# A planned packed attention and ELU feed-forward kernel: stores that count as due late, dearer accumulating stores and weight loads in the plan, a fourth weight buffer, and an order chosen anew

## The chip, the cores and the metric

The kernel runs on one core of one Trainium2 chip. The metric is the device time in microseconds (us) of one execution. A core has TensorE (PE; its weight loads are shown apart as PEld), VectorE (DVE), ScalarE (ACT), GpSimd (POOL) and SyncE (SP), each with a queue of instructions of its own that it works off in order, and sixteen DMA engines that move what the queues issue.

## The reference

There are 8 batches of 8 heads, 576 tokens, head size 64, 32 packed rows `p` a head; the feed-forward part has model size 512 and inner size 2048 over all 4608 tokens.

```python
def sm_attn(qq, kk, vv):
    s = scale * np.matmul(qq, kk.transpose(0, 1, 3, 2))
    s = s - np.max(s, axis=-1, keepdims=True)
    a = np.exp(s)
    a = a / (np.sum(a, axis=-1, keepdims=True) + 1e-09)
    return np.matmul(a, vv)
p_packed = sm_attn(p, k, v)
out = sm_attn(q, p_packed, p_packed)
...
x = out.transpose(0, 2, 1, 3).reshape(B * S, H * D)
h = x @ w_in
g = np.where(h > 0.0, h, alpha * (np.exp(np.minimum(h, 0.0)) - 1.0))
return (g @ w_out).astype(np.float32)
```

All values are float32. The kernel splits them into a high and a low part and multiplies high by high, high by low and low by high.

## The kernel before

**The work.** For each batch the kernel computes the scores of the packed rows against the keys (the "first scores"), their softmax, the product with the values (`psum<-kvq,tmp` on PE, L663), and the scores of the queries against the packed rows (L708, the "second scores"). Those are turned by DVE's 32x32 transposes (the fold, L716), go through the second softmax, and are turned back (the unfold, L758). Since the attention's output is a small matrix times the packed rows, the kernel multiplies the packed rows into `w_in` first (L809, giving `m_hi` and `m_lo`), and a token's `h` is the second softmax (`a_hi`, `a_lo`, or `q` where the unfold writes whole values) times `m`.

**The feed-forward part.** It goes over steps of a batch, a window of its tokens (256 or 320) and one of 16 blocks of 128 inner columns. A step has 12 matmuls or 6 for `h` (L1306, L1313), ELU on ACT and DVE (`e`, `g`; L1320 is its relu, L1326 its exp), and an "out group" of six matmuls with `w_out` (L1409 to L1412), whose operand has a high and a low part in `wo_a` (blocks 0 to 7) or `wo_b` (blocks 8 to 15). In batches 0 and 1 the windows are visited several times, four blocks at a time, before all weights are there. The first visit's sum is stored in `out` by SyncE; later ones are added to it by GpSimd's DMA (`accum_op`, L1455, the accumulating stores). From batch 2 on two blocks are worked off together by seven products instead of eight, which need sums of weights: these are made once (L932 to L970), stored in `sw_dram`, and loaded again for each pair (L1158), four loads of 256 KB a set. `S_PLAINS` lists the pairs that are worked off plainly, with no sums. The last 64 tokens of a batch are kept in `hb`, stored in `rest_dram` (L998) and worked off at the end.

**The weights.** A block of `w_in` or `w_out` comes as 64-bit floats, 512 KB, into a buffer of the ring `raw` (L347, SyncE). ACT lifts the uppermost bits of the low word (`up<-raw`, L342), copies them in place (`top<-up`, L320), and DVE puts the float32 word together ("whole", L367). For `w_out`, ACT then casts to the high part (`wo_a<-raw`, `wo_b<-raw`) and DVE subtracts for the low one (L381); this last one releases the buffer. There are three buffers, and L320 is the line of all casts and copies.

**What sets the order.** No order is written out. Each piece of work is an `op` with a due time (`prio`, in steps), what it costs on each engine that can do it, what it depends on, and the buffers that it takes. `schedule()` plays this forward in time: it takes the op with the earliest due time that is ready, whose buffers are free, and whose engine is idle, and writes it down. The sequence in which ops were taken is each engine's program. `"DMA"` stands for SyncE's queue and `"POOL"` for GpSimd's. The chip then goes through these programs, with semaphores where one waits for another. So a cost in the plan takes no time; it only moves instructions. The tables `T_...`, `LI`, `LO`, `LM`, `LOOK`, `TM` shift the due times of kinds of ops: `T_ATT...` those of the attention's parts, `T_SL` the loads of weight sums (due `i - T_SL` for the step `i` that uses them), `T_SE` the final sums and stores of `out`, `T_HS` the stores of `rest_dram`, `T_SW` the making of the sums.

K, v and q of batches 1 to 7 share one ring, `kvq`, of two buffers: k's two halves, then v's, then q's, each of which is loaded when the one two before it has been used.

Of the kernel before, what the change touches and what calls it, by code (L numbers as in the profile page):

```python
# [16 lines left out]
U8 = mybir.dt.uint8  # L17
# [6 lines left out]
def packed_attention_elu_ffn(  # L24
# [58 lines left out]
    ]  # L83
    T_ATT = [11.5, 5.0, 17.5, 8.0, 10.0, 14.0]
    T_ATT1 = [-17.0, -14.5, -14.0, -6.0, -18.5, -13.0]
    LI = 4.0
    LO = 2.0
    LM = 1.0
    LOOK = 4.25
    TM = [26.5, 32.5, 37.5, 36.5]  # L90
    FIRST = "q v i3 k i0 i1 i2 o2".split()
    COLD = 1.9
    T_S2 = -8.0
    STAY = 19
    SWITCH = 0.105
    F_PLAIN = 0
    H_PLAIN = [0, 1]
    T_WS = 11
    T_AS = 6
    S_PLAIN = []  # L100
    S_PLAINS = {
        (2, 0): [7], (2, 1): [0], (3, 0): [1], (3, 1): [0], (4, 0): [0, 4], (4, 1): [1],
        (5, 0): [0], (5, 1): [0], (6, 0): [4], (6, 1): [7],
    }
    T_SW7 = 36
    T_ATTS = {3: [-2.5, -1.5, -5.5, 8.5, 12.0, 21.0], 4: [-1.5, 7.5, 13.5, 3.5, 10.0, 23.0], 5: [-6.5, 4, -10.5, -3.5, 12.5, 28.0], 6: [5, 10, 14.0, 3.5, 11.5, 24.5], 7: [1.0, -10, -5, 3.5, 11.5, 23.0]}
    TMS = {3: [19, 30.0, 34.5, 30.0], 4: [22, 19.5, 26.0, 27.0], 5: [11.5, 28.5, 29.0, 29.0], 6: [23, 18.5, 28.0, 23.0], 7: [16.5, 35, 30.0, 31.5]}
    T_RL = 21.0
    T_RX = 2.0
    T_HS = 20.5  # L110
    S_FIRST = (2, 0)
    T_SW = 7.5
    T_SL = 6.5
    T_SE = 15.0
    LOOK_S = 5.5
# [54 lines left out]

    def op(prio, on, fn, deps=(), take=(), use=(), after=(), mode=None, lag=0):
        o = Op()
        o.lag = lag
        o.prio, o.on, o.fn, o.deps = prio, on, fn, [d for d in deps if d is not None]
        o.after = [d for d in after if d is not None]
        o.take, o.end, o.n, o.mode = list(take), None, len(ops), mode
        for b in list(take) + list(use):
            b.users.append(o)
        ops.append(o)
        return o  # L180

    def schedule():
# [25 lines left out]
        while todo:  # L208
            for n, o in enumerate(todo[:400]):
# [21 lines left out]
                for x, needs in o.next:  # L231
                    x.wait -= 1
                    if needs:
                        x.ready = max(x.ready, o.end)
                for r in {id(b.ring): b.ring for b in o.take}.values():
# [5 lines left out]
            else:  # L241
                ends = [o.end for o, _ in out[-400:] if o.end > now]
                ends += [t for t in idle_at.values() if t > now]
# [45 lines left out]
    for x in top_ts:  # L289
# [4 lines left out]
        kvq=2, m_hi=NFC, m_lo=NFC, a=2, tmp=3, g=3, e=2, h=2, sw=SW, w8=2, hb=HB,  # L294
        raw=3, up=2, top=TOP, p=2, ppT=2, pp=1, k0=1, q0=1,
    ).items()}
# [33 lines left out]
    def weights(f, first, prio):  # L330


        raw = ring_tile("raw", stg, [P, 8 * WC + 8], U8, "raw", bufs=3)
        up_b = ring_tile("up", stg, [P, WC], U16, "up")
# [51 lines left out]
        t = FIRST.index(name) - 60 if name in FIRST else prio - 8  # L386
        ld = op(t, {"DMA": 1.45}, load, take=[raw])
        x = op(prio, {"ACT": 0.63, "DVE": 0.42}, lift, [ld], take=[up_b], use=[raw])
# [28 lines left out]
    def attention(b, ts):  # L417
# [65 lines left out]
        def load_v(e, n):  # L483
            x = v_b[n].t
            nc.sync.dma_start(
                out=x[:, :2 * E].rearrange("p (c e) -> p c e", c=2),
                in_=v[b, 2 * n * P:2 * (n + 1) * P, :].rearrange("(c p) e -> p c e", p=P),
            )
            nc.sync.dma_start(
                out=x[:S - 4 * P, 2 * E:], in_=v[b, 4 * P:, n * E // 2:(n + 1) * E // 2]  # L490
            )

# [431 lines left out]
    def strassen_weights(u):  # L924
# [35 lines left out]
        for n, b in enumerate(sw):  # L960
            def high(e, n=n, b=b):
                copy(e, b.t[:, :H], cut(t_b, n))

            def low(e, n=n, b=b):
                nc.vector.tensor_tensor(
                    out=b.t[:, H:], in0=cut(t_b, n), in1=b.t[:, :H].bitcast(F32), op=ALU.subtract
                )

            def store(e, n=n, b=b):
                nc.sync.dma_start(out=sw_dram[u, n], in_=b.t.bitcast(F32))  # L970

# [19 lines left out]
    def keep_leftover(b, f, o, prio):  # L991
        run["hb"] = o
        hb_done[b].append(o)
        if f % 2:
# [18 lines left out]
    def strassen_pair(i, b, win, f):  # L1013
# [210 lines left out]
        if last:  # L1224
# [51 lines left out]

            op(q, {"DMA": 1.4}, store, [y], use=[part])

    acc = None
    for i, (b, win, f) in enumerate(order):  # L1280
# [140 lines left out]
        if final:  # L1421
# [25 lines left out]
            for a, (r0, r1) in zip(acc, rows):  # L1447
# [59 lines left out]
```

## Time and profile before

| | before |
|---|---|
| median of 3 runs | 708.01 us (707.46 to 708.13) |
| profiled execution | 708.88 us |
| its span | 706.3 us |
| TensorE busy | 675.5 us (96%) |
| VectorE busy | 576.3 us (82%) |
| ScalarE busy | 454.8 us (64%) |
| weight loads on TensorE | 593.9 us (84%) |
| chain that ended last, by engine | PE 83%, ACT 6%, DMA 5%, DVE 3% |

The span is that of the instructions; 2.58 us of the execution lie around it. Busy shares are averages over the whole span. They say which engine has most to do, and not where an engine waits; that is read from shorter stretches and from the rows of single instructions. In such a row stand the start in us, the duration in us, the engine, the line, the operation with out<-in, and in square brackets the idle time ahead of it and what ended it.

### The profile page before, as it was taken

What the parts mean: (1) busy time and instruction counts of PE and PEld (TensorE: products, weight loads), DVE (VectorE), ACT (ScalarE), POOL (GpSimd) and SP (SyncE); (2) the same over time, 40 slices, a digit from 0 to 9 for tenths busy, and PEclk for the clock granted to TensorE, in tenths of its full rate; (3) what the DMA queues carried; (4) which work ended last, traced back from release to release, by engine and by line L of the source; (5) the groups of instructions that cost most, each with busy time, mean ns of one, the idle gap of its engine ahead of it and who ended that gap; (6) DMA issues with size and microseconds to landing.
All of it is one profiled execution on the core that took longest, in us unless ns stands there. A gap on an engine that the chain in (4) does not pass through costs nothing.

```text
span 706.3 us, 16075 instructions
## 1 busy us (share of the span) xinstructions
PE 675.5 (96%) x6051; PEld 593.9 (84%) x6051; DVE 576.3 (82%) x1284; ACT 454.8 (64%) x888; POOL 21.1 (3%) x30
## 2 busy tenths in 40 slices
PE   3599998998999999999999999999999999999996
PEld 2376886785879988998989988898899988999996
DVE  1898665998988998778987879779986999878874
ACT  4899998785667557755674557665665566555441
POOL 0000011102010000000000000000000000000000
PEclk9889999999999999999999999999999999999999
DMA  8877777579399956969788777798788787675863
GB/s 324 279 238 248 237 196 153 122 203 290 125 268 295 314 182 199 318 194 312 245 262 267 242 212 231 240 274 270 250 285 299 224 274 235 194 219 158 293 206 124
DMA packets 102797, 167.79 MB, mean 238 GB/s; under 512 B 26176, under 2 KB 35392, under 8 KB 102464
## 3 DMA queue, kind: packets, MB, share of 16 engines
q1 hardware_dynamic: 99552, 160.99, 70.5%
q0 software_dynamic: 3168, 5.77, 5.3%
q8 instruction: 48, 0.79, 0.4%
q14 instruction: 29, 0.24, 0.1%
HBM read 138.94 MB, written 27.79 MB: 236 GB/s over the span
## 4 chain that ended last, share of the span: by engine, by line
PE 83%; ACT 6%; DMA 5%; DVE 3%; issue 1%; SPq 1%; DVEq 0%; ACTq 0%
PE psum L1200 40%; PE psum L1044 22%; PE psum L809 4%; PE psum L1313 4%; PE psum L1409 3%; PE psum L1410 2%; PE psum L1412 2%; DMA raw<-in_w_out 2%; PE psum L663 2%; DMA raw<-in_w_in 1%; PE psum L1306 1%; DMA kvq<-in_qT 1%; PE psum L708 1%; PE psum L637 1%; PE psum L567 1%
## 5 line engine op out<-in xcount | busy, mean ns | idle before, releaser
L1200 PE MATMUL psum<-sw,g 128*128 128x256 f32 x1212 | 183.7, 283 | 0.0
L1200 PEld LDWEIGHTS psum<-sw,g 128*128 128x128 f32 x1212 | 160.7, 189 | 9.5 <-issue 7.0
L1135 DVE TENSOR_TENSOR g<-w,g 128x896 fp32r<-128x896 f32 (+1 forms) x96 | 99.6, 1039 | 28.4 <-ACT g L320 28.0
L320 ACT CAST g<-w 128x896 fp32r<-128x896 f32 (+1 forms) x96 | 86.6, 903 | 52.9 <-PE psum L1200 23.4
L1044 PE MATMUL psum<-a_hi,m_hi 128*128 128x256 f32 (+1 forms) x384 | 115.5, 301 | 0.0
L1044 PE MATMUL psum<-a_hi,m_lo 128*128 128x256 f32 (+1 forms) x384 | 113.5, 296 | 0.0
L1044 PE MATMUL psum<-a_lo,m_hi 128*128 128x256 f32 (+1 forms) x384 | 113.4, 295 | 0.0
L1200 PE MATMUL psum<-wo_a,g 128*128 128x256 f32 (+1 forms) x537 | 90.7, 299 | 0.4 <-ACT e L1059 0.4
L1126 DVE TENSOR_TENSOR w<-w 128x128 f32<-128x128 f32 (+1 forms) x255 | 84.8, 333 | 6.4
L1200 PE MATMUL psum<-wo_b,g 128*128 128x256 f32 (+1 forms) x534 | 84.8, 288 | 0.0
L1200 PEld LDWEIGHTS psum<-wo_a,g 128*128 128x128 f32 x537 | 75.9, 189 | 5.8 <-issue 1.8
L1044 PEld LDWEIGHTS psum<-a_hi,m_hi 128*128 128x128 f32 x384 | 72.7, 189 | 8.7 <-issue 2.7
L1056 ACT ACTIVATE e<-psum 128x320 f32<-128x320 f32 x96 | 41.7, 436 | 57.4 <-PE psum L1044 54.9
L1200 PEld LDWEIGHTS psum<-wo_b,g 128*128 128x128 f32 x534 | 73.1, 189 | 4.5 <-issue 3.4
L1044 PEld LDWEIGHTS psum<-a_lo,m_hi 128*128 128x128 f32 x384 | 72.6, 189 | 0.2
L1044 PEld LDWEIGHTS psum<-a_hi,m_lo 128*128 128x128 f32 x384 | 72.6, 189 | 0.0
L1056 ACT ACTIVATE w<-psum 128x512 f32<-128x512 f32 x48 | 28.6, 598 | 41.4 <-PE psum L1044 23.4
L1051 DVE SCALAR_TENSOR_TENSOR w<-e,psum 128x256 f32<-128x256 f32 x96 | 39.8, 415 | 15.8 <-ACT e L1059 15.5
L1059 ACT ACTIVATE e<-e 128x320 f32<-128x320 f32 x96 | 45.1, 472 | 2.6
L822 DVE TENSOR_TENSOR m_lo<-psum,m_hi 128x1024 fp32r<-128x1024 f32 (+1 forms) x36 | 37.1, 1038 | 7.1 <-ACT m_hi L320 7.1
L1051 DVE SCALAR_TENSOR_TENSOR w<-w,psum 128x512 f32<-128x512 f32 x48 | 32.5, 678 | 10.5 <-ACT w L1059 10.3
L320 ACT CAST m_hi<-psum 128x1024 fp32r<-128x1024 f32 (+1 forms) x36 | 31.1, 875 | 12.0 <-PE psum L809 11.3
(121 smaller groups left out, 1156.7 us busy)
## 6 DMA issues: line engine op xcount, KB each, us to landing
sw<-sw_dram SPq DMA_DIRECT2D x340, 256.0 KB, 3.9
raw<-in_w_in SPq DMA_DIRECT2D x16, 512.0 KB, 4.6
kvq<-in_v SPq DMA_DIRECT2D x16, 512.0 KB, 5.7
raw<-in_w_out SPq DMA_DIRECT2D x16, 512.0 KB, 4.8
out<-part SPq DMA_DIRECT2D x32, 256.0 KB, 3.4
sw_dram<-sw SPq DMA_DIRECT2D x32, 256.0 KB, 5.5
kvq<-in_kT SPq DMA_DIRECT2D x14, 576.0 KB, 5.0
kvq<-in_qT SPq DMA_DIRECT2D x14, 576.0 KB, 5.5
```

The costliest lines, as they stand in the source:

```text
L320: (nc.scalar.copy if e == "ACT" else nc.vector.tensor_copy)(out=out, in_=in_)
L809: nc.tensor.matmul(ps.t[cols_of(pair), g, :w], lhsT=st.ppT.t[rows_of(g), pair, :], rhs=w_in_sb[rows_of(g), pair, c * FC + part * w:c * FC ...
L822: nc.vector.tensor_tensor(out=m_b[1].t[:, :, fs], in0=ps.t[:, :, :w], in1=m_b[0].t[:, :, fs].bitcast(F32), op=ALU.subtract,)
L1044: nc.tensor.matmul(ps, lhsT=m_b[p].t[:, g, o:o + P], rhs=st.a.t[q][:, g, cols], start=(n == 0), stop=(n == 3 * G - 1),)
L1051: nc.vector.scalar_tensor_tensor(out=out, in0=e_, scalar=-1.0, in1=ps, op0=ALU.add, op1=ALU.max)
L1056: nc.scalar.activation(out=out, in_=ps, func=AF.Relu, scale=-1.0)
L1059: nc.scalar.activation(out=x, in_=x, func=AF.Exp, scale=-1.0)
L1126: nc.vector.tensor_tensor(out=out, in0=x, in1=y, op=o)
L1135: nc.vector.tensor_tensor(out=g_b.all[:, 7 * P:(7 + b1 - b0) * P], in0=blocks(b0, b1), in1=g_b.all[:, :(b1 - b0) * P].bitcast(F32), op=ALU ...
L1200: nc.tensor.matmul(a.t[:, at * H:at * H + rhs.shape[-1]], lhsT=operand(blk, p), rhs=rhs, start=new and n == k == 0, stop=a.final == (u, mi ...
L1313: nc.tensor.matmul(ps_b.t[:, :n_tok], lhsT=m_b[x].t[:, g, o:o + P], rhs=st.a.t[y][:, g, cols], start=(n == 0), stop=(n == 3 * G - 1),)
L1409: nc.tensor.matmul(a.t, lhsT=g_b.t[0][:, t], rhs=wo(f, 0), start=first, stop=False)
```

## The change

The plan gets other costs, other due times, and one more buffer; one input is laid out in another way.

- `LATE`: what depends on a store (of `sw_dram`, `rest_dram`, `out`) becomes ready 1.5 us later in the plan.
- An accumulating store, which took 1.0 of GpSimd's time in the plan, now takes 1.7 of the DMA lane's, with 2.8 more until it has ended. It is still issued by GpSimd.
- A weight load ends 0.4 later in the plan; a store of `rest_dram` takes 0.3 instead of 0.5.
- The ring `raw` has four buffers.
- The host lays v out as one block of 128 rows a half, padding included, so that a half is one DMA instead of two.
- The due times are new, and in `S_PLAINS` window (2, 0) has two plain pairs instead of one.

```diff
+    LATE = 1.5
-    T_ATT = [11.5, 5.0, 17.5, 8.0, 10.0, 14.0]
+    T_ATT = [15.5, -5.0, 17.5, 11.5, 10.5, 14.0]
...
-        (2, 0): [7], (2, 1): [0], (3, 0): [1], (3, 1): [0], (4, 0): [0, 4], (4, 1): [1],
-        (5, 0): [0], (5, 1): [0], (6, 0): [4], (6, 1): [7],
+        (2, 0): [0, 7], (2, 1): [0], (3, 0): [1], (3, 1): [0], (4, 0): [0, 4], (4, 1): [0],
+        (5, 0): [0], (5, 1): [1], (6, 0): [4], (6, 1): [7],
...
-    T_SL = 6.5
+    T_SL = -2.5
...
-                        x.ready = max(x.ready, o.end)
+                        x.ready = max(x.ready, o.end + x.late)
...
-        raw=3, up=2, top=TOP, p=2, ppT=2, pp=1, k0=1, q0=1,
+        raw=4, up=2, top=TOP, p=2, ppT=2, pp=1, k0=1, q0=1,
...
-        raw = ring_tile("raw", stg, [P, 8 * WC + 8], U8, "raw", bufs=3)
+        raw = ring_tile("raw", stg, [P, 8 * WC + 8], U8, "raw", bufs=4)
...
-        ld = op(t, {"DMA": 1.45}, load, take=[raw])
+        ld = op(t, {"DMA": 1.45}, load, take=[raw], lag=0.4)
...
         def load_v(e, n):
-            x = v_b[n].t
-            nc.sync.dma_start(
-                out=x[:, :2 * E].rearrange("p (c e) -> p c e", c=2),
-                in_=v[b, 2 * n * P:2 * (n + 1) * P, :].rearrange("(c p) e -> p c e", p=P),
-            )
-            nc.sync.dma_start(
-                out=x[:S - 4 * P, 2 * E:], in_=v[b, 4 * P:, n * E // 2:(n + 1) * E // 2]
-            )
+            nc.sync.dma_start(out=v_b[n].t, in_=v[b, n])
...
-            s_ready[u, n] = op(prio, {"DMA": 0.7}, store, [y], use=[b])
+            s_ready[u, n] = op(prio, {"DMA": 0.7}, store, [y], use=[b], late=LATE)
...
-            rest_done[b, f // 2] = op(prio - T_HS, {"DMA": 0.5}, store, hb_done[b], use=[x])
+            rest_done[b, f // 2] = op(
+                prio - T_HS, {"DMA": 0.3}, store, hb_done[b], use=[x], late=LATE
+            )
...
-            op(q, {"DMA": 1.4}, store, [y], use=[part])
+            op(q, {"DMA": 1.4}, store, [y], use=[part], late=LATE)
...
-                eng = {"POOL": 1.0} if visits[v_n][2] > 0 else {"DMA": 0.7}
-                stores[r0] = op(i + LOOK, eng, store, [y, stores.get(r0)], use=[part])
+                again = visits[v_n][2] > 0
+                stores[r0] = op(
+                    i + LOOK, {"DMA": 1.7 if again else 0.7}, store, [y, stores.get(r0)], use=[part],
+                    lag=2.8 * again, late=LATE,
+                )
```

Lines move by a few: the lift is L342 before and L343 after, casts L320 and L321, whole L367 and L368, the fold L716 and L710, the unfold L758 and L752, the second scores L708 and L702, relu and exp L1320, L1326 and L1316, L1322, out groups L1409 to L1412 and L1405 to L1408.

Three places show what the new plan does. The first is DVE's program from the first fold of batch 1 on, some 20 us into the span. Before:

```order
10 L716 STREAM_TRANSPOSE tmp<-psum 128x288 x2
11 L723 TENSOR_REDUCE mx_286<-tmp 128x18
12 L726 TENSOR_TENSOR tmp<-tmp,mx_286 128x576
13 L367 SCALAR_TENSOR_TENSOR raw<-raw,top 128x512
14 L736 TENSOR_REDUCE sm_306<-tmp 128x18
15 L381 TENSOR_TENSOR wo_a<-raw,wo_a 128x512
16 L739 TENSOR_SCALAR sm_306<-sm_306 128x18
17 L742 RECIPROCAL sm_306<-sm_306 128x18
18 L745 TENSOR_TENSOR tmp<-tmp,sm_306 128x576
19 L758 STREAM_TRANSPOSE k_335<-tmp 128x2x288
```

and after:

```order
14 L720 TENSOR_TENSOR tmp<-tmp,mx_290 128x576
15 L530 TENSOR_REDUCE mx<-psum 128x1
16 L730 TENSOR_REDUCE sm_332<-tmp 128x18
17 L538 TENSOR_SCALAR nb<-mx 128x1
18 L530 TENSOR_REDUCE mx<-psum 128x1
19 L733 TENSOR_SCALAR sm_332<-sm_332 128x18
20 L736 RECIPROCAL sm_332<-sm_332 128x18
21 L538 TENSOR_SCALAR nb<-mx 128x1
22 L368 SCALAR_TENSOR_TENSOR raw<-raw,top 128x512
23 L739 TENSOR_TENSOR tmp<-tmp,sm_332 128x576
24 L368 SCALAR_TENSOR_TENSOR raw<-raw,top 128x512
25 L752 STREAM_TRANSPOSE k_366<-tmp 128x2x288
```

Two weight words (L368) and two maxima of the next batch's scores (L530) have moved ahead of the first unfold. From the first fold to the last unfold of that part DVE has the same 82 instructions in both.

The second is ACT's program ahead of a weight's lift in the steps of batches 0 and 1, near 115 us of the trace before. There the row `wo_b<-raw` is the cast whose buffer, three weights back, the lift in the last row has to wait for:

```order
192 L320 CAST wo_b<-raw 128x512
193 L1320 ACTIVATE e<-psum 128x320
194 L320 CAST top<-up 128x512
195 L1326 ACTIVATE e<-e 128x320
196 L320 CAST m_hi<-psum 128x2x256
197 L1320 ACTIVATE e<-psum 128x320
198 L342 ACTIVATE up<-raw 128x512
199 L1326 ACTIVATE e<-e 128x320
200 L320 CAST top<-up 128x512
201 L320 CAST g<-e 128x256 x2
202 L342 ACTIVATE up<-raw 128x512
```

The same load's lift is the last row of this part of the program after:

```order
186 L1316 ACTIVATE e<-psum 128x320
187 L343 ACTIVATE up<-raw 128x512
188 L1322 ACTIVATE e<-e 128x320
189 L1316 ACTIVATE e<-psum 128x320
190 L321 CAST top<-up 128x512
191 L321 CAST g<-e 128x256
192 L1322 ACTIVATE e<-e 128x320
193 L321 CAST wo_b<-raw 128x512
194 L321 CAST g<-e 128x256
195 L321 COPY part<-psum 128x512
196 L1316 ACTIVATE e<-psum 128x320
197 L343 ACTIVATE up<-raw 128x512
```

With four buffers the buffer of this load was last used four weights back, by the word made from the `top` in ACT's row 179; 17 rows lie between that and the lift.

The third is PE's program ahead of the second scores of batch 2, near 170 us of the trace before. An out group reads `wo_b`. Before:

```order
497 L1409 MATMUL psum<-wo_b,g 128x512
498 L1410 MATMUL psum<-wo_b,g 128x512
499 L1409 MATMUL psum<-wo_b,g 128x512
500 L1410 MATMUL psum<-wo_b,g 128x512
501 L1412 MATMUL psum<-wo_b,g 128x512 x2
502 L708 MATMUL psum<-kvq,ppT 32x288 x8
503 L809 MATMUL psum<-w_in_sb,ppT 32x512 x8
504 L708 MATMUL psum<-kvq,ppT 32x288 x8
505 L809 MATMUL psum<-w_in_sb,ppT 32x512 x8
```

After:

```order
520 L1405 MATMUL psum<-wo_b,g 128x512
521 L1406 MATMUL psum<-wo_b,g 128x512
522 L1405 MATMUL psum<-wo_b,g 128x512
523 L1406 MATMUL psum<-wo_b,g 128x512
524 L1408 MATMUL psum<-wo_b,g 128x512 x2
525 L1405 MATMUL psum<-wo_b,g 128x512
526 L1406 MATMUL psum<-wo_b,g 128x512
527 L1405 MATMUL psum<-wo_b,g 128x512
528 L1406 MATMUL psum<-wo_b,g 128x512
529 L1408 MATMUL psum<-wo_b,g 128x512 x2
530 L702 MATMUL psum<-kvq,ppT 32x288 x16
```

Two out groups stand directly ahead of the second scores instead of one, and the products with `w_in` (L809) no longer stand between the halves. Beyond the named places, the last weight's word is put together at about the 29th step instead of the 33rd.

More of the change, by code (lines that the diff above doesn't have):

```diff
@@ L83, in packed_attention_elu_ffn @@
     ]
-    T_ATT = [11.5, 5.0, 17.5, 8.0, 10.0, 14.0]
[L85 to L91, printed above, removed]
+    T_ATT = [15.5, -5.0, 17.5, 11.5, 10.5, 14.0]
+    T_ATT1 = [-11.5, -17.0, -21.0, -6.0, -18.5, -18.5]
+    LI = 5.0
+    LO = 2.5
+    LM = 0.0
+    LOOK = 5.25
+    TM = [29.5, 32.5, 37.5, 37.0]
+    FIRST = "v i3 q k i0 i1 i2".split()
     COLD = 1.9
-    T_S2 = -8.0
+    T_S2 = -9.5
     STAY = 19
@@ L97, in packed_attention_elu_ffn @@
     H_PLAIN = [0, 1]
-    T_WS = 11
-    T_AS = 6
+    T_WS = 26
+    T_AS = 4
     S_PLAIN = []
     S_PLAINS = {
-        (2, 0): [7], (2, 1): [0], (3, 0): [1], (3, 1): [0], (4, 0): [0, 4], (4, 1): [1],
-        (5, 0): [0], (5, 1): [0], (6, 0): [4], (6, 1): [7],
-    }
[L105 to L110, printed above, removed]
+        (2, 0): [0, 7], (2, 1): [0], (3, 0): [1], (3, 1): [0], (4, 0): [0, 4], (4, 1): [0],
+        (5, 0): [0], (5, 1): [1], (6, 0): [4], (6, 1): [7],
+    }
+    T_SW7 = 33
+    T_ATTS = {3: [-2.5, -1.5, -4.5, 8.5, 11.5, 21.0], 4: [-1.5, 7.5, 12.5, 4.0, 10.0, 25.0], 5: [-7.0, 4.5, -13.0, -3.5, 12.5, 28.0], 6: [5, 10, 14.0, 1.5, 11.5, 24.5], 7: [1.0, -5.5, -5, 3.5, 11.0, 25.0]}
+    TMS = {3: [18, 29.5, 34.5, 30.0], 4: [22, 19.5, 26.0, 27.0], 5: [11.5, 28.5, 28.5, 28.0], 6: [23, 18.5, 29.0, 23.0], 7: [16.5, 35.5, 30.0, 31.5]}
+    T_RL = 17.0
+    T_RX = 1.0
+    T_HS = 25.0
     S_FIRST = (2, 0)
-    T_SW = 7.5
-    T_SL = 6.5
-    T_SE = 15.0
+    T_SW = 20.5
+    T_SL = -2.5
+    T_SE = 21.5
     LOOK_S = 5.5
@@ L169, in packed_attention_elu_ffn, with op @@
     LAG = {"PE": 0.27, "DVE": 0.05, "ACT": 0.05, "DMA": 2.2, "POOL": 5.0, "CTL": 0.0}
-    def op(prio, on, fn, deps=(), take=(), use=(), after=(), mode=None, lag=0):
+    def op(prio, on, fn, deps=(), take=(), use=(), after=(), mode=None, lag=0, late=0):
         o = Op()
-        o.lag = lag
+        o.lag, o.late = lag, late
         o.prio, o.on, o.fn, o.deps = prio, on, fn, [d for d in deps if d is not None]
@@ L241, in schedule @@
             else:
-                ends = [o.end for o, _ in out[-400:] if o.end > now]
+                ends = [o.end + t for o, _ in out[-700:] for t in (0, LATE) if o.end + t > now]
                 ends += [t for t in idle_at.values() if t > now]
@@ L1484, in pairs_T, with values @@
         )
+    def values(x):
+        out = np.zeros((B, 2, 128, 2 * E + E // 2), x.dtype)
+        for n in range(2):
+            for c in range(2):
+                out[:, n, :, c * E:(c + 1) * E] = x[:, (2 * n + c) * 128:(2 * n + c + 1) * 128]
+            out[:, n, :S - 512, 2 * E:] = x[:, 512:, n * E // 2:(n + 1) * E // 2]
+        return out
     arrays = {
@@ L1488 @@
         "in_kT": pairs_T(k),
-        "in_v": np.ascontiguousarray(v.transpose(0, 2, 1, 3).reshape(B, S, H * D)),
+        "in_v": values(v.transpose(0, 2, 1, 3).reshape(B, S, H * D)),
         "in_pT": pairs_T(p),
```

## The prediction

> **What bounds the kernel now.** I read the page's head first, then the busy times by stretches of 20 us, then, where TensorE was not full, the chain that ended last and the rows of single instructions. From the page:
>
> ```profile
> span 706.3 us, 16075 instructions
> PE 675.5 (96%) x6051; PEld 593.9 (84%) x6051; DVE 576.3 (82%) x1284; ACT 454.8 (64%) x888; POOL 21.1 (3%) x30
> PEclk9889999999999999999999999999999999999999
> ```
>
> TensorE is busy for 675.5 of 706.3 us, so some 31 us are all that a better order can win, plus what a lower clock costs (slices 2 and 3). The stretches say where those lie. Columns: the stretch, its length, busy us and instructions of PE, weight loads, DVE, ACT and POOL, the granted clock, the DMA share, GB/s.
>
> ```profile
> 0.00:20.00 20.00, 7.95 (x147) 5.25 (x155) 4.36 (x11) 10.44 (x21) 1.62 (x8) 0.99 0.82 303
> 20.00:40.00 20.00, 13.96 (x189) 8.94 (x172) 18.37 (x38) 16.16 (x36) 0.00 (x0) 0.76 0.85 284
> ...
> 60.00:80.00 20.00, 19.07 (x112) 14.45 (x113) 15.22 (x34) 19.97 (x47) 0.00 (x0) 1.00 0.65 215
> 80.00:100.00 20.00, 20.00 (x121) 16.93 (x119) 14.16 (x34) 19.97 (x48) 1.91 (x2) 1.00 0.76 203
> 100.00:120.00 20.00, 16.94 (x102) 13.90 (x100) 11.34 (x31) 15.96 (x38) 2.58 (x4) 0.97 0.66 183
> 120.00:140.00 20.00, 20.00 (x173) 16.17 (x174) 18.54 (x43) 15.58 (x38) 4.44 (x6) 0.95 0.64 123
> 160.00:180.00 20.00, 17.73 (x210) 12.39 (x209) 16.88 (x39) 11.89 (x29) 3.62 (x4) 0.91 1.00 285
> 620.00:640.00 20.00, 20.00 (x163) 20.00 (x163) 14.97 (x36) 10.96 (x19) 0.00 (x0) 1.00 0.72 210
> ```
>
> PE lacks 12.05 and 6.04 us in the first 40, 0.93 at 60 to 80, 3.06 at 100 to 120 and 2.27 at 160 to 180. From 180 on it looks like the last row: 20.00 of 20 at full clock, which no order of the same matmuls can shorten. ACT is full (19.97 of 20) from 60 to 100. So the change can act in three places: the start, the hole near 118 (A) and the one near 173 (B).
>
> **The start.** The order there holds the same work on DVE in another sequence. The next two rows are the stretch from DVE's first fold to its last unfold of batch 1, and the matmul that waits for that unfold:
>
> ```profile
> 20.45:60.37 39.92, 33.07 (x344) 21.88 (x326) 37.49 (x82) 34.77 (x77) 0.00 (x0) 0.88 0.82 273
> 60.43 1.88 PE L1306 MATMUL psum<-q,m_hi 128*128 128x320 f32 x6 [0.88 <-DVE q L758]
> ```
>
> DVE is busy 37.49 of 39.92 us, and the matmul at 60.43 sat 0.88 us for it. DVE sets the end of this stretch. The changed order has the same 82 instructions there, so it can win at most the idle 2.43 us. It can lose: the first unfold now comes behind two weight words and two maxima more. Lateness of DVE's own items does not lengthen a chain that is full, but it can open a gap behind PE; I bound that by the wait already there plus its like, about +1.5. I take the middle of -2.4 and +1.5, -0.5 us.
>
> **A, the weight load near 118.** The chain, then the rows of DVE, ACT, POOL and PE, the clock by 5 us, the landing times of the raw loads between 85 and 125, and the two DMA queues of the page:
>
> ```profile
> 108.40 6.49 DMA raw<-in_w_out
> ...
> 107.68 0.69 DVE L381 TENSOR_TENSOR wo_b<-raw,wo_b 128x512 fp32r<-128x512 f32 x1
> ...
> 114.91 0.65 ACT L342 ACTIVATE up<-raw 128x512 uint16<-128x512 uint8 x1 [2.99 <-DMA raw<-in_w_out]
> ...
> 117.87 0.36 PE L1313 MATMUL psum<-a_hi,m_hi 128*128 128x256 f32 x1 [2.51 <-ACT up L342]
> ...
> 106.59 1.75 POOL L1455 DMA_DIRECT2D out<-part  x2 [11.14 <-ACT part L320]
> ...
> 115.00:120.00 5.00, 2.44 (x13) 1.84 (x12) 2.34 (x7) 5.00 (x12) 0.82 (x2) 0.86 0.31 116
> 120.00:125.00 5.00, 5.00 (x25) 4.28 (x25) 3.98 (x8) 4.66 (x12) 0.93 (x2) 0.80 0.88 121
> ...
> DMA to landing us min/median/max: 3.6/5.2/6.6
> ...
> q1 hardware_dynamic: 99552, 160.99, 70.5%
> q0 software_dynamic: 3168, 5.77, 5.3%
> ```
>
> DVE frees the raw buffer at 108.37, SyncE issues the load into it at 108.40, it lands 6.49 us later, and ACT, which wanted it at 111.92, waits 2.99; PE then waits 2.51 for ACT. An accumulating pair had left at 106.59. Such stores are dear: 5.3% of 706.3 us for 22 of 256 KB is 1.70 us of all sixteen DMA engines each, against 0.81 for 256 KB of the ordinary queue (70.5% of 706.3 over 160.99 MB).
>
> A costs 3.06 us of PE idle (20 - 16.94). Then the clock: its means of 0.97 and 0.95 over 20 us each are 0.6 + 1.0 us, and the two 5 us rows show that most of it lies right behind the gap. A = 4.66 us. The Trainium skill, in "TensorE: Matmul & The Clock Gate", section "What's actually happening", says the half-rate state follows about one idle window of 3.4 us. This trace does not agree: after a gap of 2.51 us the granted clock was 0.80 to 0.86. By that rule A would be worth 3.06 us and B, below, 2.27, and the sum 2.6 us less (704.4); since the clock rows speak against it, it gets no chance of its own.
>
> With a fourth raw buffer, the load waits for the weight before that. In the old order nine rows of ACT lie between the cast that frees the buffer and the lift; they took 3.5 us (108.4 to 111.92), 0.39 a row. In the new order 17 rows lie between the release and the same lift: 17 x 0.39 = 6.6 us, as long as the slowest landing, 6.6. ACT then goes on, and PE is not late at its rate. The tightest earlier load keeps about 12 rows, 4.8 us, against the median of 5.2: about 0.5 us of wait left. A is worth -4.2 (ends: -4.66, and 0 where ACT's queue has no room, below).
>
> **B, the queries of batch 2.** K, then v, then q of a batch use the same two buffers, so q's halves leave when the first product with v is done, and the second softmax's scores wait for them. The chain, the PE rows around it, and the clock:
>
> ```profile
> 165.76 7.47 DMA kvq<-in_qT
> ...
> 163.58 1.46 PE L663 MATMUL psum<-kvq,tmp 128*32 128x64 f32 x80
> 164.97 0.38 PE L1313 MATMUL psum<-a_hi,m_hi 128*128 128x256 f32 x1
> 165.78 0.40 PE L1409 MATMUL psum<-wo_b,g 128*128 128x512 f32 x1
> 167.18 0.27 PE L689 MATMUL psum<-ident,pp 128*128 128x128 f32 x1
> 169.51 0.72 PE L708 MATMUL psum<-kvq,ppT 64*32 64x288 f32 x16
> 173.37 1.21 PE L708 MATMUL psum<-kvq,ppT 64*32 64x288 f32 x16 [2.27 <-DMA kvq<-in_qT]
> ...
> 170.00:175.00 5.00, 2.73 (x48) 0.94 (x40) 4.51 (x10) 2.79 (x6) 1.76 (x2) 0.82 1.04 361
> 175.00:180.00 5.00, 5.00 (x37) 3.42 (x22) 2.54 (x6) 2.70 (x5) 0.00 (x0) 0.84 1.03 275
> ```
>
> The second half lands at 173.23, 8.26 us after the product's end at 164.97; PE waited 2.27. The clock of 0.91 over 20 us costs 1.8. B = 4.07 us. Before the scores there were 4.54 us of cover (164.97 to 169.51). The new order puts a second out group in, 1.40 us (165.78 to 167.18), so the cover is 5.94, and 6.4 to the second half. If that half lands as before, the wait is 1.8; if a load takes 6.7 (the median of v's loads below), 0.3. I take 1.05, so 1.22 of 2.27 goes and the same share of the clock's 1.8: -2.2.
>
> What is late next is v. Its last old issue and the landing of the loads between 148 and 152:
>
> ```profile
> 151.46 0.53 SPq L489 DMA_DIRECT2D kvq<-in_v  x1
> ...
> DMA to landing us min/median/max: 5.1/6.7/7.9
> ```
>
> The four old loads left between 149.1 and 151.5, so the last was there by 159.4 at the latest, 10.3 us after the buffers came free; PE first wanted it at 163.58. In the new order less work lies between the keys' scores and this product: three out groups (4.2), 24 matmuls of 256 columns at 0.12 (20 us / 163 in the last window above: 2.9) and a few transposes, 7.5 to 8 us. But v is now one DMA a half instead of two, so two issues fall away, and the second leaves some 0.6 us after the first. At the median it lands at 7.3 and nobody waits; at 10.3 the wait is 2.3. I take +0.3. B nets -1.9, from -4.1 to +2.3.
>
> **The rest.** One more plain pair at (2,0) replaces products on weight sums: 33 matmuls of 256 columns fewer and 18 of 512 more, 3 x 0.12 = +0.4 us, which PE pays in full. Four loads of weight sums fewer, hidden: 0. Casts that change between ACT and DVE, beyond 180 us: 0, PE covers them (10.96 and 14.97 busy of 20). Later due times of stores: 0, unless the last rival holds.
>
> Sum: -0.5 - 4.2 - 1.9 + 0.4 = -6.2. The profiled execution took 708.88 us, 2.58 of them around its span of 706.3, and lies 0.87 over the median of 708.01. Against the median: **701.8 us**.
>
> **The rivals.**
> 1. ACT is the bound of A, not the load. For it: ACT had 19.97 of 20 us twice ahead of A, and the new order finishes the weights' conversion about four steps earlier, so their lifts and tops (0.65 us a row) must go where ACT is full. Four rows more ahead of the step at A are 2.6 us, and PE would come late by nearly that. Against it: casts of g go to DVE, which has 14 to 15 of 20 busy there; by counting, ACT's rows up to that step grow by one or two only. If all of A stays: 708.0 - 0.5 - 1.9 + 0.4 = 706.0.
> 2. B is not relieved: q's landing stretches with the cover, or v comes late by 2.3 in place of q's wait. The DMA share was 1.04 there, so the engines were full, and the sums' stores now stand further ahead. By "DMA: Bandwidth & Descriptors", section on queues, rings and completion order, the Trainium skill has each DMA engine switch between the rows by packets, so that an accumulating store would take share from q; no run here separates that. B at about 0: 708.0 - 0.5 - 4.2 + 0.4 = 703.7.
> 3. All is covered: -2.4 - 4.66 - 4.07 + 0.4 = -10.7, 697.3.
> 4. Nothing is won: waits move to other loads one for one; 708.0.
> 5. Slower. The loads of weight sums are due nine steps later than before. They run on SyncE's queue, where they can stand behind a store that waits:
>
> ```profile
> SPq L998 <- DVE w L1126: 23.9, 29, 2.5
> ...
> PEld psum L1200 <- DMA sw<-sw_dram: 1.7, 2, 0.8
> ...
> sw<-sw_dram SPq DMA_DIRECT2D x340, 256.0 KB, 3.9
> ```
>
> Before, the queue stood 23.9 us in 29 waits of that kind, yet the weight loads waited for sums only 1.7 us in 2. There are 84 sets of four loads; if each came 0.15 us late, PE would lose 12.6: 714.4. It decides from (6.2 + 1.4) / 84 = 0.09 us a set. Against it: in the order, the PE work between a load's place and its use is at least 6.4 us in both kernels, over the 3.9 of a landing.
>
> **Chances.** Forecast 0.51, rival 1 0.13, rival 2 0.15, rival 3 0.07, rival 4 0.07, rival 5 0.07. A measurement of this kernel can tell about 0.2%, 1.4 us, from no change. Faster by more: the forecast, rivals 2 and 3 and most of rival 1 (706.0 is 2.0 below, with an uncertainty of its own: 0.08 of 0.13), 0.81. Within: rival 4 and the rest of rival 1, 0.12. Slower: 0.07. The range: from 697.6, all covered but for 0.3, to 706.6, rival 1 with 0.6 of the start's upside lost. It leaves out rivals 4 and 5 and about 0.05 beyond the lower end.
>
> **What would show it.** In the new profile: PE over 19.5 of 20 in 100 to 120 with a clock of 0.99 or more, no lift that waits over 1 us for raw (A); the scores of batch 2 waiting about 1 us for q, the product with v under 0.5 (B); the first matmul on folded queries at 59 to 61 (the start); 20.00 of 20 from 180 on. I am wrong if PE waits for sums after 180, if ACT's own rows, not a DMA, end PE's idle time near 118, or if PE's idle time in the first 60 us grows by over 1.5.

## The result

The changed kernel took 702.39 us (median of 4 runs, 701.77 to 704.28) against 708.07 (707.46 to 709.32): a ratio of 0.9922, with a 95% interval of 0.9898 to 0.9946. The forecast was 701.8. The profiled execution took 701.77 us with a span of 699.9, against 708.88 and 706.3.

The head of the page after, answering to the three lines shown of before:

```profile
span 699.9 us, 15989 instructions
...
PE 675.2 (96%) x6036; PEld 592.1 (85%) x6036; DVE 574.2 (82%) x1282; ACT 453.8 (65%) x887; POOL 21.1 (3%) x30
...
PEclk9899999999999999999999999999999999999999
```

TensorE's busy time is the same within 0.3 us, so by this count the time that went was waiting. A matmul at a lower clock counts as busy, so the clock is read beside it. The stretches of the trace after say where, in the columns known from before:

```profile
0.00:20.00 20.00, 8.59 (x139) 5.39 (x147) 4.44 (x11) 10.81 (x22) 1.62 (x8) 1.00 0.91 345
20.00:40.00 20.00, 16.69 (x215) 10.28 (x206) 18.77 (x40) 18.21 (x41) 0.00 (x0) 0.83 0.89 322
...
80.00:100.00 20.00, 19.96 (x106) 16.83 (x105) 14.09 (x34) 20.00 (x49) 1.92 (x2) 1.00 0.72 193
100.00:120.00 20.00, 19.75 (x121) 16.55 (x120) 16.27 (x42) 18.48 (x45) 3.48 (x4) 1.00 0.68 142
120.00:140.00 20.00, 20.00 (x160) 15.89 (x159) 19.86 (x50) 14.20 (x37) 3.46 (x4) 1.00 0.81 214
...
160.00:180.00 20.00, 19.46 (x203) 15.64 (x202) 19.12 (x46) 12.85 (x35) 1.76 (x2) 1.00 1.02 324
```

The hole near 118 is gone (19.75 of 20 busy where it was 16.94), the one near 173 has shrunk from 2.27 us to 0.54, and the granted clock is 1.00 in the stretches from 100 to 140 and 160 to 180, where it had been 0.97, 0.95 and 0.91. In the trace after, the raw load that had come late was issued at 101.42 and lifted without a wait at 109.99. SyncE's row and ACT's:

```profile
101.42 0.55 SPq L348 DMA_DIRECT2D raw<-in_w_out  x1
109.99 0.68 ACT L343 ACTIVATE up<-raw 128x512 uint16<-128x512 uint8 x1
```

In the list of waits (total us, times, longest) one wait of ACT for raw is left in the whole program:

```profile
ACT up L343 <- DMA raw<-in_w_in: 2.1, 1, 2.1
```

And the raw loads between 85 and 125 us landed faster at the slow end, 5.7 instead of 6.6:

```profile
DMA to landing us min/median/max: 4.3/4.7/5.7
```

At batch 2, PE now waits a little for v and a little for q. The chain shows the two loads:

```profile
154.45 7.95 DMA kvq<-in_v
...
164.19 6.06 DMA kvq<-in_qT
```

The rows of PE show the waits:

```profile
162.44 1.01 PE L657 MATMUL psum<-kvq,tmp 128*32 128x64 f32 x48 [0.17 <-DMA kvq<-in_v]
170.39 0.72 PE L702 MATMUL psum<-kvq,ppT 64*32 64x288 f32 x16 [0.37 <-DMA kvq<-in_qT]
```

The matmul that waits for the last unfold of batch 1 starts at 58.83 instead of 60.43. On the other side, two short waits late in the span are new, where a store of `rest_dram` or a chain of DVE's sums holds `hb` (before has one short wait late in the span, 0.35 us at 605):

```profile
58.83 2.42 PE L1302 MATMUL psum<-q,m_hi 128*128 128x320 f32 x8 [1.07 <-DVE q L752]
...
450.93 0.41 PE L1040 MATMUL psum<-a_hi,m_hi 128*128 128x320 f32 x1 [0.31 <-DVE hb L1047]
...
597.45 0.38 PE L1040 MATMUL psum<-a_hi,m_hi 128*128 128x320 f32 x1 [0.76 <-DVE hb L1047]
```

To size the stages, I lined the traces up by the matmul work done so far (each shape at its spacing in full stretches) and took the lead over before at the same work. The two other columns are experiments told below. Each column rests on one execution. That of before took 708.88 us, while the medians of its four sets lie between 706.66 and 708.07, so the leads in the last row are larger than the differences of the medians (5.7, 4.2 and 4.3 us).

| time in before, us | lead of after | fourth buffer alone | plain stores alone |
|---|---|---|---|
| 61 | 1.6 | 1.6 | 0.3 |
| 111 (ahead of A) | 1.1 | 2.0 | 0.6 |
| 131 (behind A) | 5.3 | 5.1 | 4.8 |
| 167 (ahead of B) | 5.0 | 4.8 | 4.4 |
| 186 (behind B) | 7.7 | 6.2 | 6.0 |
| 238 | 8.3 | 5.9 | 6.0 |
| 424 | 8.5 | 5.9 | 6.1 |
| last matmul | 7.4 | 5.9 | 6.1 |
| span | 6.4 | 5.9 | 6.1 |

So A gave 4.2 us and B 2.7; the start 1 to 1.6; 1.1 was given back late, and some of the rest behind the last matmul. A second trace of the changed kernel, from a later run told below, lined up in the same way, has a lead of 0.7 at 61, 0.1 ahead of A, 4.3 behind it and 4.7 at the last matmul. A's 4.2 repeats; the other stages are not firm to a microsecond.

### The profile page after: what moved, and what is told of

Its sections match the earlier page's. It is cut to its first block, busy times and chain, and to the rows that moved or that the text cites. A ratio compares the mean times of both kernels' runs of the same rounds, so it can differ in the third digit from the quotient of the medians.

```text
span 699.9 us, 15989 instructions
## 1 busy us (share of the span) xinstructions
PE 675.2 (96%) x6036; PEld 592.1 (85%) x6036; DVE 574.2 (82%) x1282; ACT 453.8 (65%) x887; POOL 21.1 (3%) x30
## 4 chain that ended last, share of the span: by engine, by line
PE 79%; ACT 8%; DMA 5%; DVE 5%; issue 1%; SPq 0%; DVEq 0%; ACTq 0%
PE psum L1196 39%; PE psum L1040 22%; PE psum L803 4%; PE psum L1309 3%; PE psum L1405 2%; PE psum L1406 2%; PE psum L1408 2%; ACT top L321 2%; PE psum L657 1%; ACT up L343 1%; DMA kvq<-in_v 1%; PE psum L702 1%; ACT e L1322 1%; ACT e L1316 1%; PE psum L631 1%
## 5 line engine op out<-in xcount | busy, mean ns | idle before, releaser
L1196 PE MATMUL psum<-sw,g 128*128 128x256 f32 x1200 | 181.2, 282 | 0.0
L1196 PEld LDWEIGHTS psum<-sw,g 128*128 128x128 f32 x1200 | 158.9, 189 | 7.0 <-issue 2.7
L321 ACT CAST g<-w 128x896 fp32r<-128x896 f32 (+1 forms) x96 | 86.3, 899 | 45.8 <-DVE w L1122 22.5
L1196 PE MATMUL psum<-wo_a,g 128*128 128x256 f32 (+1 forms) x540 | 92.1, 301 | 0.0
L321 ACT CAST m_hi<-psum 128x1024 fp32r<-128x1024 f32 (+1 forms) x36 | 31.0, 874 | 9.5 <-PE psum L803 6.4
```

The lines of the kernel that those rows point to most:

```text
L321: (nc.scalar.copy if e == "ACT" else nc.vector.tensor_copy)(out=out, in_=in_)
L1196: nc.tensor.matmul(a.t[:, at * H:at * H + rhs.shape[-1]], lhsT=operand(blk, p), rhs=rhs, start=new and n == k == 0, stop=a.final == (u, mi ...
```

## The experiments

The question was which part brings this: the buffer, the order, the dearer stores in the plan, or the layout of v. Each run was compared with the kernel before on the same chip.

**The fourth buffer alone, in the order of before.** Only the pool that makes the buffers changes; the plan still counts three, so every engine's program is the same row for row.

```diff
-        raw = ring_tile("raw", stg, [P, 8 * WC + 8], U8, "raw", bufs=3)
+        raw = ring_tile("raw", stg, [P, 8 * WC + 8], U8, "raw", bufs=4)
```

> The order of before, word for word, with four raw buffers on the chip where the plan still counts three. Theory (the hole near 118 is a weight load that waits for its buffer): the load leaves one weight earlier, ACT's waits for raw (9.9 us in 6 before) fall under 2, the hole is gone and the clock there stays at 1.00: -4.2 us, 703.9 against 708.1; the start and B stay. Rival (ACT's own work sets PE there, since it is full from 60 to 100): ACT's waits go, but PE's idle time near 118 stays; 707 to 708.

Measured: 702.46 us against 706.66, 0.9933 (0.992 to 0.9947). The stretches around A and, last, the one of B:

```profile
100.00:120.00 20.00, 19.50 (x119) 16.39 (x118) 13.43 (x32) 18.71 (x44) 3.51 (x4) 1.00 0.73 173
120.00:140.00 20.00, 19.88 (x185) 14.91 (x184) 19.82 (x49) 15.12 (x38) 3.51 (x4) 1.00 0.59 120
...
160.00:180.00 20.00, 17.61 (x161) 13.55 (x154) 18.22 (x41) 12.55 (x31) 1.77 (x2) 1.00 0.86 253
```

What is left of ACT's waits for raw:

```profile
ACT up L342 <- DMA raw<-in_w_in: 2.2, 1, 2.2
ACT up L342 <- DMA raw<-in_w_out: 1.3, 2, 1.0
```

The second scores of batch 2 on PE:

```profile
165.54 0.72 PE L708 MATMUL psum<-kvq,ppT 64*32 64x288 f32 x16 [0.78 <-DMA kvq<-in_qT]
168.74 0.72 PE L708 MATMUL psum<-kvq,ppT 64*32 64x288 f32 x16 [1.61 <-DVE sw L965]
```

The hole is gone, with PE at 19.50 of 20 and the clock at 1.00. ACT's waits fell from 9.9 us to 3.5, not under 2 as expected. The raw loads between 85 and 125 us took about as long to land as before (5.0 us at the median, 7.1 at most), so it is the earlier issue that closed the hole. ACT's own work, full ahead of A, did not set PE: the first rival of the prediction falls, but for a wait of 0.49 us for ACT at 114.79. By the table A gave 3.1 us here. At B the wait for q shrank, though nothing of B was edited, but a wait of 1.61 for DVE stood behind it: 2.39 us together, no less than the 2.27 of before, and PE's busy time from 160 to 180 is no larger (17.61 against 17.73). The lead still grew by 1.4 there, because the clock stayed at 1.00 instead of 0.91. The expectation had the start and B unchanged.

**Three buffers in the order of after.** The same line the other way round.

```diff
-        raw = ring_tile("raw", stg, [P, 8 * WC + 8], U8, "raw", bufs=4)
+        raw = ring_tile("raw", stg, [P, 8 * WC + 8], U8, "raw", bufs=3)
```

> The order of after, word for word, with three raw buffers on the chip. Theory: this order was laid out for four; with three, four of the later lifts stand only 1.3 to 3 us of ACT's work behind the release of their buffer, against a landing of 4.7, so ACT waits about 10 us more and PE pays from half to most of it: 706 to 711 against 702.4. Rival (the new order alone relieves A, the buffer is spare): 702.4 within 1.

Measured: 727.18 us against 706.66, 1.0281 (1.0259 to 1.0304): 25 us over the changed kernel, far beyond the 4 to 9 expected. The stretch where PE lost most:

```profile
20.00:40.00 20.00, 9.60 (x95) 4.88 (x91) 15.30 (x33) 13.97 (x28) 0.00 (x0) 0.58 0.63 227
```

ACT's waits for raw:

```profile
ACT up L343 <- DMA raw<-in_w_out: 11.2, 4, 4.9
ACT up L343 <- DMA raw<-in_w_in: 8.0, 4, 2.8
```

SyncE's rows for one weight load and for batch 1's v behind it, in the trace after:

```profile
23.27 0.33 SPq L348 DMA_DIRECT2D raw<-in_w_in  x1
24.16 1.10 SPq L485 DMA_DIRECT2D kvq<-in_v  x2
```

and with three buffers:

```profile
34.17 0.33 SPq L348 DMA_DIRECT2D raw<-in_w_in  x1
34.59 0.86 SPq L485 DMA_DIRECT2D kvq<-in_v  x2
```

ACT waits 19.2 us for raw instead of 2.1. What the expectation left out is the queue: SyncE issues in order, so a weight load that has no buffer holds what stands behind it. Here v left 10.4 us later, directly behind a weight load that left 10.9 later. PE was idle for over half of the stretch from 20 to 40, and the clock was 0.50 from 23 to 47 us. Lined up with the trace after, some 9 us were lost by 40 us, 16 by 80, and all 25 by 105, which is ahead of A. What each held load cost is not separated. The order needs its buffer; but its loss lies ahead of A, so this run is no second test of A.

**The layout of v, both ways.** In before, one DMA a half; in after, two as before.

```diff
-            x = v_b[n].t
-            nc.sync.dma_start(
...
+            nc.sync.dma_start(out=v_b[n].t, in_=v[b, n])
```

> Before with the new layout of v alone: one DMA a half of 640 KB with its padding instead of two of 576 KB together; the order of everything else is that of before. Theory: v of batch 2 was not waited for, and B starts from the end of the product, so the time stays: 708.1 within 0.7. Rival (fewer issues free SyncE, and later loads, q's too, land earlier): 1 to 2 us faster. Second rival (padding takes DMA time from q): 0.5 to 1 slower.

> After with the old layout of v alone, two DMAs a half. Theory: the cover of v at batch 2 is about 9 us in the new order and v lands 9.1 after the scores' end as it is; two issues more of 0.5 us each make it 1 us later, and PE waits 1 us there and loses some clock: 703.4 to 704.4 against 702.4. Rival (the layout is worth nothing): 702.4 within 0.7.

Measured: 1.0008 (0.9997 to 1.002) for the first: nothing. The second gave 0.9954 (0.9941 to 0.9966), where the changed kernel gave 0.9922 and 0.9921 in its two sets, so the old layout may cost the new order 1.3 us by the medians (703.73 and 702.39) or 2.3 by the ratios; the intervals touch, so it is not shown. The median lies in the range expected. Its trace shows 1.40 us of wait for q and 0.38 for v at batch 2, against 0.37 and 0.17:

```profile
162.28 1.01 PE L664 MATMUL psum<-kvq,tmp 128*32 128x64 f32 x48 [0.38 <-DMA kvq<-in_v]
171.26 0.72 PE L709 MATMUL psum<-kvq,ppT 64*32 64x288 f32 x16 [1.40 <-DMA kvq<-in_qT]
```

The wait was expected at v and stands mostly at q, one load later in the same two buffers.

**The changed kernel again, beside the buffer and the layout in the old order.** The second kernel joins the two edits shown, and nothing of the plan.

> The changed kernel once more, beside the next three on one chip. Theory (the fourth buffer alone makes the gain, as it did in the order of before with a ratio of 0.9933; the new order adds next to nothing): 0.992, at most 1 us below the next run. Rival (the order is worth the difference at B that the traces show, 1.6 us, and keeps it): 1.5 us or more below the next run.

> The order of before with the fourth buffer on the chip and the new layout of v; plan, costs and tables of before. Theory (the layout is worth nothing by itself): 0.993, as with the buffer alone. Rival (it shortens the waits for v and q of batch 2 by the 0.5 to 1 us that the run with the old layout in the new order lost): 0.992, level with the run before.

Measured: 0.9921 (0.9895 to 0.9947) and 0.9911 (0.9884 to 0.9937), 702.39 and 701.98 us. Two edits that leave the order alone do as much as the whole change. The lead that the new order has over the buffer alone, 1.5 us behind B and 2.4 at 238 us, is lost again between 424 us and the end but for 0.5.

**What the plan does with the buffer.** If the buffer alone is worth 0.67%, a plan that counts it should keep that. Three kernels vary the plan: counting four buffers with all else of before; the changed kernel with all tables of before; and the new tables with before's costs and three buffers.

```diff
-        raw=3, up=2, top=TOP, p=2, ppT=2, pp=1, k0=1, q0=1,
+        raw=4, up=2, top=TOP, p=2, ppT=2, pp=1, k0=1, q0=1,
```

> Before with four buffers on the chip and in the plan, with the costs and tables of before. The same buffer with the order left alone gave 0.9933; the new costs with old tables gave 0.9965. Theory (a plan that counts the buffer runs loads and lifts earlier, and only the order of the rest changes): 0.993 to 0.996. Rival (the late stores and dear accumulating stores in the plan were what cost c1 its 2 us): 0.992 to 0.993.

> The changed kernel with all tables of before (due times, FIRST, the plain pairs): the costs, the late stores, four buffers in the plan, and the layout of v stay. Theory (any plan that knows four buffers relieves A; the tables matter by less than 1.5 us): 0.992 to 0.995. Rival (tables and costs fit only together, and the old ones open new waits): over 0.997.

> Before with the tables of the changed kernel alone: three buffers in the plan and on the chip, the costs of before, two DMAs a half of v. Theory (without the fourth buffer the weight loads wait, whatever the tables): ACT waits for raw about as long as before or longer, 707 to 712 against 707. Rival (the tables move the lifts away from the releases, and three buffers do): 703 to 705.

Measured: 1.0001 (0.9987 to 1.0014), 0.9965 (0.9949 to 0.9981), and 1.0262 (1.0238 to 1.0286); no trace of the last is read here. The first is the surprise, outside both ranges expected: counted in the plan, the same buffer is worth nothing. Its trace has no hole at A either, but two others, in the stretches

```profile
60.00:80.00 20.00, 16.46 (x80) 11.84 (x80) 15.33 (x33) 19.60 (x45) 0.00 (x0) 1.00 0.68 218
...
180.00:200.00 20.00, 17.85 (x118) 14.54 (x117) 15.28 (x36) 10.06 (x22) 1.75 (x2) 0.91 0.60 169
```

and in the rows of PE:

```profile
66.07 1.31 PE L1306 MATMUL psum<-q,m_hi 128*128 128x320 f32 x4 [1.89 <-ACT wo_a L320]
...
186.94 0.42 PE L1313 MATMUL psum<-a_hi,m_hi 128*128 128x320 f32 x1 [1.97 <-DVE e L1329]
```

PE waits 1.89 us for ACT just behind a cast `wo_a`, with ACT full there (19.60 of 20), and 1.97 for DVE's part of ELU behind a softmax. The waits moved from a load to the engines. That the plan, with a free buffer, puts weight casts ahead of work that PE needs sooner is my reading of these two waits; no run tests it. The new costs, with the layout of v, bring back half (0.9965), the new tables the other half (0.9921); the 0.9965 lies between its two ranges. That the tables alone, with three buffers, are some 19 us slower than before, far over the 707 to 712 expected, agrees with the run on three buffers above.

**Which tables.** The changed kernel with before's tables from batch 2 on, and with before's tables up to batch 1:

```diff
-    T_SL = -2.5
-    T_SE = 21.5
+    T_SL = 6.5
+    T_SE = 15.0
```

(with them `S_PLAINS`, `T_SW7`, `T_ATTS`, `TMS`, `T_RL`, `T_RX`, `T_HS`), or

```diff
-    LI = 5.0
-    LO = 2.5
-    LM = 0.0
-    LOOK = 5.25
+    LI = 4.0
+    LO = 2.0
+    LM = 1.0
+    LOOK = 4.25
```

(with them `T_ATT`, `T_ATT1`, `TM`, `FIRST`, `T_S2`, `T_SW`).

> The changed kernel with the tables of before for what comes from batch 2 on (plain pairs, the attention's due times from batch 3 on, loads of sums, leftovers, final sums); the tables of the start and of the first two batches stay new. Theory (the new order gives back about 1.4 us late: two waits at 450 and 597 us, 0.7 more than before, and an end 0.7 longer): 1 to 1.5 us below the changed kernel, PE idle from 180 on below 0.5. Rival (that is chance between runs): the same within 0.7.

> The changed kernel with the tables of before for the start and the batches 0 and 1, and its own tables from batch 2 on. With new early and old late tables the ratio was 0.9921, with both old 0.9965. Theory (only the early tables matter, since 60 to 180 us hold the waits): 0.996. Rival (it is the pair of both that counts): 0.992 to 0.994.

Measured: 0.9921 (0.9893 to 0.9949) and 0.9933 (0.9919 to 0.9946), level with the changed kernel. My theory that the old late tables would win 1 to 1.5 us fell: they removed the wait of 0.76 and opened one of 1.24 us at another batch's scores.

```profile
469.30 0.72 PE L702 MATMUL psum<-kvq,ppT 64*32 64x288 f32 x16 [1.24 <-DMA kvq<-in_qT]
```

That the early tables alone matter, the theory of the second run at 0.996, fell too. Either half of the tables can be old; with both old 2 to 3 us are lost (0.9949 to 0.9981 against 0.9919 to 0.9946). The run with both old has before's `T_AS` as well, a due time of ops in batches 0 and 1 that neither half changes, so the loss need not come from the pair. No single table was shown to matter.

**The price of the accumulating stores.** The prediction gave them twice an ordinary store's DMA time and could not say what that does to A. This kernel is before with one argument left out, so `out` lacks the earlier visits' sums:

```diff
-                        nc.gpsimd.dma_start(out=out[r0:r1, :], in_=part.t, accum_op=ALU.add)
+                        nc.gpsimd.dma_start(out=out[r0:r1, :], in_=part.t)
```

> Before with the 22 later visits' stores written plainly by GpSimd's queue instead of added, so the sums in out lack the earlier visits; order, queue and bytes stay. Theory of the prediction (an accumulating store takes twice the DMA time of another and stretches the landing of 6.5 us that made A): the landing falls by about 1 us, ACT's wait for raw near 112 to about 2, 706 against 707. Rival (the landing is long for its own 512 KB and the traffic beside it): no difference within 0.7.

Measured: 703.04 us against 707.31, 0.9934 (0.9919 to 0.995), four times the expected 1 us. The page's row of that queue (packets, MB, share of the sixteen engines):

```profile
q0 software_dynamic: 1760, 5.77, 2.1%
```

The landing of the raw loads between 85 and 125 us:

```profile
DMA to landing us min/median/max: 3.5/4.0/4.5
```

ACT's waits for raw, and the lift at A:

```profile
ACT up L342 <- DMA raw<-in_w_out: 3.1, 3, 1.5
ACT up L342 <- DMA raw<-in_w_in: 2.1, 1, 2.1
...
111.10 0.68 ACT L342 ACTIVATE up<-raw 128x512 uint16<-128x512 uint8 x1 [0.35 <-DMA raw<-in_w_out]
```

The stretches at A:

```profile
100.00:120.00 20.00, 19.80 (x122) 17.15 (x123) 14.13 (x36) 19.65 (x47) 2.14 (x4) 1.00 0.58 196
120.00:140.00 20.00, 19.96 (x186) 15.10 (x185) 19.81 (x48) 15.15 (x38) 2.16 (x4) 1.00 0.30 111
```

The scores at B on PE:

```profile
168.86 0.72 PE L708 MATMUL psum<-kvq,ppT 64*32 64x288 f32 x16 [2.07 <-DMA kvq<-in_qT]
```

The 22 stores now take 2.1% of the engines instead of 5.3% (0.67 us for 256 KB instead of 1.70), the raw loads land in 4.0 us at the median and 4.5 at most instead of 5.2 and 6.6. The load of A left at 107.21 and its lift waited 0.35 us at 111.10, instead of 2.99, so A closes with three buffers: 4.2 us by the table, as much as in the changed kernel and more than the 3.1 of the buffer alone. So A had two causes that were both needed: a buffer that came free late, and a landing stretched by an accumulating pair. Either cure is enough, and the fourth buffer is the one that keeps the sums. At B the wait for q stayed (2.07), so there the accumulating pair is not the cause, and the second rival's store that takes share from q is not borne out. The lead grew by 1.6 at B all the same: the clock stayed at 1.00.

## Why the prediction was right

- **What bounds it.** That only the start, A and B could give anything held: TensorE's busy time is unchanged and the clock rows are 1.00 where the holes were.
- **A: -4.2 forecast, -4.2 measured.** The step "with a fourth raw buffer, the load waits for the weight before that" is shown by the buffer alone, which closes the hole in the old order (3.1 of the 4.2). The 0.5 us of wait that I kept did not come. My price of an ACT row was low: the nine rows that I timed from the buffer's release had begun ahead of it, and from 107.51 to 111.92 they took 4.4 us, 0.49 a row instead of 0.39. In the trace after, 8.6 us lie between the load's issue and its lift, where I had 6.6. The part "PE is not late at its rate" held although ACT is full; the rival that it is not, at 706.0, was wrong.
- **The cause of the landing.** The prediction put the accumulating stores beside A and gave no number to it. They were the whole difference between a landing that the old distance covers and one that it does not.
- **B: -1.9 forecast, -2.7 measured.** I took q's landing as 7.4 us from the product's end; the second half landed 6.8 after it, at 170.25, and PE waited 0.37 instead of 1.05. Waits for v of 0.17 us at the product came as forecast (0.3). The cover that I put at 5.94 us was 5.9 (163.45 to 169.31); that the second out group made it is read from the order, and no run isolates it. The clock's share went completely rather than in proportion to the wait. With the buffer alone and with the plain stores it went too, though the waits were about as long as before. There it was chance, as the last section shows.
- **The start: -0.5 forecast, 1.1 to 1.6 won.** Within the 2.4 allowed, and not shown to be the order's doing: the buffer alone has the same lead of 1.6 at 61 us, and the changed kernel's second trace has 0.7. The stretch from DVE's first fold to its last unfold of batch 1, 39.92 us with DVE busy 37.49 before, is in the trace after and, second, with the buffer alone:

```profile
20.41:58.78 38.37, 33.88 (x347) 21.98 (x331) 36.69 (x82) 35.66 (x79) 0.00 (x0) 0.91 0.76 264
...
20.44:58.82 38.38, 31.24 (x347) 20.87 (x331) 37.07 (x82) 34.58 (x76) 0.00 (x0) 0.96 0.80 272
```

  It is 1.5 us shorter in both. In the trace after, half of that is DVE's idle time (1.68 instead of 2.43) and half is the busy time of the same 82 instructions. The first fold starts within 0.04 us in all three, so the first wait for the keys, which moved between 7.4 and 9.3 us among the kernels' traces, is not the cause here. Why both orders are shorter stays open.
- **The rest: 0 forecast.** Not so: 2 us of the lead of 8.5 at 424 us are gone at the end. Waits of 0.31 and 0.76 us, against 0.35 before, are 0.7 of it, and the time behind the last matmul, 6.3 us instead of 5.7, another 0.7. The extra matmuls of the plain pair, which the lining-up counts only at the end, were forecast at 0.4. The rival of late weight sums is the nearest to this, but the waits are for `hb` and for DVE, not for `sw`, and are a tenth of its size.
- **What the forecast hid.** The sum was right, partly by luck: the start and B gave more than forecast and the end took about as much back. Its attribution to the order was not right. A kernel with the old order, the buffer and the layout is as fast (701.98 against 702.39 us), and none of the kernels run was shown to be faster than the changed one.

## What to carry to other kernels

Before a plan is made anew, try its one new resource in the old order: here one number in one line was worth 0.67%, and the same number told to the plan was worth nothing until costs and due times were fitted again. A load that comes late has a distance and a landing, and both are worth a test: taking the neighbouring transfers' cost away closed the hole as well as one more buffer did. An in-order queue makes a missing buffer dear: here v stood 10 us behind a weight load without a buffer.

## What the runs showed of the hardware

**Accumulating stores.** An accumulating store of 256 KB took 1.70 us of all sixteen DMA engines, the same store written plainly from the same queue 0.67 us. The landings of the raw loads between 85 and 125 us went with it, from 4.0 to 5.2 us at the median and from 4.5 to 6.6 at most.

**The clock after a gap.** I charged the clock as if each hole of over 2 us cost it. The traces show more when they are cut where the clock changes: it is 1.00 or 0.50, and a stretch at 0.50 inside the program lasts 3.41 us or a multiple. The 0.80 to 0.91 of the longer rows are means of the two. In before, the steps of 3.41 us with the gap of 2.51 at A and behind it:

```profile
115.21:118.62 3.41, 0.90 (x7) 0.78 (x6) 1.64 (x5) 3.41 (x9) 0.00 (x0) 1.00 0.39 151
118.62:122.03 3.41, 3.36 (x12) 2.78 (x11) 2.35 (x6) 3.41 (x9) 1.75 (x2) 0.50 0.52 47
```

With the plan that counts four buffers, around the gap of 1.97 that starts at 185.0:

```profile
184.52:187.93 3.41, 1.44 (x11) 1.23 (x11) 3.38 (x7) 1.73 (x5) 0.00 (x0) 1.00 0.76 244
187.93:191.34 3.41, 3.41 (x12) 2.82 (x11) 2.18 (x7) 0.91 (x2) 0.00 (x0) 0.50 0.20 76
```

And with the plain stores, on that trace's own steps, around the gap of 2.07 that starts at 166.8:

```profile
164.29:167.71 3.42, 2.40 (x36) 0.93 (x34) 3.35 (x10) 2.98 (x7) 1.07 (x2) 1.00 0.84 217
167.71:171.12 3.41, 2.26 (x38) 1.34 (x39) 2.45 (x4) 1.24 (x3) 0.00 (x0) 1.00 1.07 411
171.12:174.53 3.41, 3.41 (x20) 2.92 (x20) 2.92 (x7) 2.15 (x6) 0.00 (x0) 1.00 0.97 367
```

The first two gaps lie within one step, and the next step is at 0.50. The third falls on a border: PE is idle 1.02 us in one step and 1.15 in the next, and the clock stays. With the buffer alone, the two waits of B leave 1.83 us idle in the fullest step (165.12 to 168.53), and the clock stays too. So what counts is the idle time within a step, not the length of the gap. From 60 us on, every step with 1.97 us idle or more was followed by 0.50, so also those with 2.14 (B in before) and 3.08 (before with the new layout of v, 116.27 to 119.68). Steps with up to 1.83 were not, except one of 1.74 in the new order on three buffers (70.83 to 74.25). In the first 60 us both outcomes occur from 1.5 to 1.9, so no sharp limit is shown. One step at 0.50 costs a busy TensorE up to 1.7 us, an estimate as half of 3.41. Before pays it at A and at B; where a gap falls on the steps is chance, and other executions of before had a mean clock of 0.983 to 0.997, against 0.987 in its trace.

The Trainium skill, in "TensorE: Matmul & The Clock Gate", section "What's actually happening", says that the window over which activity is watched runs free of the kernel. The traces agree: the changed kernel's two traces have their first step at 0.50 at 27.95 and at 19.49 us, 8.46 apart, which is no multiple of 3.41. The section's figure of about 3.4 us of idleness does not fit the steps with 1.97 to 2.51 us idle.
